# Half-size products of the output projection in another order, first layernorm rows in halves, weight sums from tiles already on chip, and self-checks at the end of the next matrix product

## Chip, cores and metric

One core of one Trainium2 chip. The metric is the device time of one execution in microseconds (us), lower is better. The kernel before took 1502.25 us, the median of three runs (1499.3 to 1504.81).

The engines named below are TensorE (PE, matrix products), VectorE (DVE), ScalarE (ACT), GpSimd (POOL) and SyncE (SP, which only issues DMAs). ACT and POOL issue DMAs too. Each engine executes its own list of instructions in order and waits for others through semaphores.

## The reference

A transformer layer on 2048 tokens of width 1024, with a recurrent attention of 32 heads of 128 (64 segments of 32 tokens, 8 memory rows carried from one segment to the next), and a feed-forward part. All six modulation rows come from a vector `c`.

```python
h = _layernorm(x) * (1 + ca) + sa
# attention by segments: tokens [mem(8) | 32 rows], q, k, v by Wq, Wk, Wv, masked softmax,
# o = heads @ Wo ; mem = o[:, :8] for the next segment ; output o[:, 8:]
x = x + ga * A(h, mem0, Wq, Wk, Wv, Wo)
h = _layernorm(x) * (1 + cb) + sb
h1 = _gelu(_layernorm(h) @ w1)
hs = shifted_quarters(h1) @ w2
x1 = h + hs
x = x + gb * (x1 + _gelu(_layernorm(x1) @ w3) @ w4)
```

So the token rows pass through Wo (4096 x 1024), a residual sum, two layernorms one after the other, then w1, w2, w3 and w4.

## The kernel before

Up to about 790 us the attention runs. Head pairs `hp` are projected by `P_units`, whose pieces fill the gaps between pieces of the attention of the pair before. For each pair, `load_wo2` brings the 256 rows of Wo into a tile `wo2`; `M_units` multiplies them with the memory rows of the heads and adds into `Macc` (L717 to L721). A second list of pieces, `guard_units`, reads w3 and w4 through a single tile, squares them on ACT (the squares' sums go into a check), and in between reads Wo once more, pair by pair: `wo_sums` forms four differences of its 512-wide blocks with four DVE subtractions and stores them through GpSimd's queue to `WoT_d` (L699). The heads' outputs of the tokens, transposed, go to `OTw_d` (L779).

The Wo product of the tokens follows, in two waves of 1024 tokens each. A wave computes a 2 by 2 block product with seven half-size products instead of eight (Winograd's form of Strassen's algorithm), in the order `ORDER`. A product is two halves `hf` of the 4096-deep sum, and a half is four units `i`, each 8 matmuls 128x128 by 128x512 into one PSUM bank (L970). The left operands are the token blocks A11, A12, A21, A22 and three sums of them, formed by DVE in place on SBUF slots (`X_sum`, `sums`; one sum of a half is 128 x 4096 fp16). The right operands are quarters of Wo or the sums in `WoT_d`; `b_upto` loads them, half a product at a time, through a ring of four tiles on SP's queue, ahead of the unit that calls it. `load_a` loads the token blocks on the same queue.

Two families of PSUM banks take part: `b` (pools of `acc_tile`) is opened by product 1 and is the target of 1, 6, 7 and 4; `d` (pool `psB`, four banks) is opened by 2 and again by 5, and is the target of 2, 5 and 3. After the second half of a product, `after(j, i)` takes results out: `snap` (L930) is an ACT copy of 128x512 to SBUF, `fin` (L936, L937) a DVE add of a bank and a snapshot and a DVE multiplication by `ga`, which gives half a row tile of x1. Before a unit may open a bank again, all readers of the bank must be done.

Row tiles (128 tokens, 8 in a wave) then pass through `C1a`: xt, the rows of x, comes in on SP's queue (L1102), GpSimd adds it (L1103), ACT's queue stores x1 (L1105), `ln_act` normalizes: DVE statistics (L106 to L110; their result for the first layernorm lies in `ves`), rstd on GpSimd (L112), one small DVE operation, one ACT operation (L1093) that makes u. DVE scales and shifts u (L1108, L1109), it is stored, and a second `ln_act` makes z, which `C1b` brings transposed into `zTs` by a DMA on ACT's queue. `chain(t0)` makes four row tiles, one lagging behind the other, and `interleave` weaves it between products: tiles 0 to 3 with the last two products of wave 0, 4 to 7 with the first three of wave 1, 8 to 11 with its last two, 12 to 15 with the first two blocks of w1.

w1 is four blocks `A_units(b)` of 512 tokens, eight units of eight matmuls each (L1182), with a gelu on ACT (L1183). Blocks 0 and 1 read `zTs[0]`, 2 and 3 `zTs[1]`; as the rows are shifted by 32 tokens, block 2 also needs the first z of tile 12, and block 3 needs all up to tile 15. w2 follows (from 1086 us), then w3 and w4.

Two self-checks run on the way. `check_a` compares the memory rows' result in eight rounds (GpSimd, ACT squares, GpSimd: L1043 to L1047), between products 3 and 6 of wave 0. `check_b` sums up over limits on the softmax's denominators, on the squares of w3 and w4, on `ves` and others, with a matmul at its end (L1082) between the second and the third block of w1; its flag goes to the host's side as an output.

The compiler's scheduler orders the instructions of each engine by estimated readiness and by the order in which the program creates them, up to the w3 and w4 part, whose order is written out. The order of allocation of ring tiles and pool buffers follows the program.

Of the kernel before, what the change touches and what calls it, by code (L numbers as in the profile page):

```python
# [60 lines left out]
def kernel(ctx, tc, A_x, A_mem0, A_Wq, A_Wk, A_Wv, A_Wo, A_seg_len, B_x, B_w1, B_w2, B_w3, B_w4, c, w_mod, out,  # L61
# [41 lines left out]
    def layernorm_stats(pool, src, ve=None):  # L103
        st = pool.tile([P, 2, 6], F32, name="ln_st")
        for i in range(2):
            nc.vector.bn_stats(out=st[:, i, :], in_=src[:, i * 512:(i + 1) * 512])  # L106
# [62 lines left out]
    def first_pass(late_hook):  # L169
# [53 lines left out]
        wop = LM.enter_context(tc.tile_pool(name="up_wo", bufs=2))  # L223
        otmp = LM.enter_context(tc.tile_pool(name="up_otm", bufs=2))
# [315 lines left out]
        wsp = LX.enter_context(tc.tile_pool(name="x_ws", bufs=1))  # L540
        rowp = LX.enter_context(tc.tile_pool(name="up_row", bufs=1))
        ws_pools[:] = [wsp]
        state = {}
# [6 lines left out]
        def load_wo2(hp):  # L550
            wo2 = wop.tile([P, 2, D], BF16, name="wo2")
            nc.sync.dma_start(wo2[:], Wo2[hp * 256:hp * 256 + 256, :].rearrange("(h p) n -> p h n", p=P))
            state["wo2", hp] = wo2

# [72 lines left out]
        def P_units(hp):  # L627
# [8 lines left out]
            ms = M_units(hp - 3) if hp >= 3 else []  # L636
            units = []
            for s in range(3):
# [8 lines left out]
                units += ms[s:s + 1]  # L647
# [20 lines left out]
        def guard_units():  # L668
# [32 lines left out]
            for i in range(28):  # L701
                units += [load(i), nop, nop, square(i)]
                if i % 7 in (0, 2, 4, 6):
                    k = i // 7 * 4 + i % 7 // 2
                    units += [wo_load(k), nop, nop, wo_sums(k)]
# [132 lines left out]
        NHP = H // 2  # L838
# [38 lines left out]
        def slot(nm):  # L877
# [3 lines left out]
                 {(0, 0): "s3", (0, 1): "s4", (1, 0): "s0", (1, 1): "s2", "X": "s1"}]  # L881
# [15 lines left out]
        ORDER = (1, 2, 5, 3, 6, 7, 4)  # L897
# [21 lines left out]
        def wave(w):  # L919
# [5 lines left out]
            def x1_new(t):  # L925
                x1s[t] = xpools["tp4"].tile([P, D], F32, name="x1")

# [5 lines left out]
            def fin(t, n, acc, s=None):  # L933
# [3 lines left out]
                nc.vector.tensor_tensor(x1s[t][:, cs], (acc if s is None else s)[:], ga_b[:, cs], ALU.mult)  # L937

            def after(j, i):
# [3 lines left out]
                elif j == 2:  # L943
                    x1_new(t1)
# [3 lines left out]
                elif j == 6:  # L948
                    fin(t1, 1, x["d"], snap("st2", x["b"]))
                elif j == 7:  # L950
                    x1_new(t2)
# [4 lines left out]
            def unit(j, hf, i):  # L956
                def f():
                    if i == 0:
                        b_upto(seq.index((w, j, hf)) + 3)
# [11 lines left out]
                    if hf:  # L971
                        after(j, i)
                return f

            def X_sum(hf):
                def f():
                    ks = slice(8 * hf, 8 * hf + 8)
                    nc.vector.tensor_tensor(f16(open_a(w, "X")[:, ks]), Av[w, (1, 0)][:, ks], Av[w, (1, 1)][:, ks], ALU.add)
                return f

            def sums(hf):
                def f():
                    ks = slice(8 * hf, 8 * hf + 8)
                    A11, A12, A21, X = (Av[w, key][:, ks] for key in ((0, 0), (0, 1), (1, 0), "X"))
                    nc.vector.tensor_tensor(f16(A21), A11, A21, ALU.subtract)
                    nc.vector.tensor_tensor(f16(A11), f16(X), A11, ALU.subtract)
# [3 lines left out]
            U[2][4:4] = [X_sum(0)]  # L990
            U[2].append(X_sum(1))
            U[5][6:6] = [sums(0)]
            U[5].append(sums(1))
            return U

        U0 = wave(0)
# [3 lines left out]
        b_upto(3)  # L1000
        load_a(0, (0, 1), 1)
# [7 lines left out]
        b_upto(5)  # L1009
        load_a(0, (1, 0), 1)  # L1010
        for h, t in ((H - 2, 0), (H - 1, 0), (H - 2, 1)):
            nc.vector.tensor_copy(Av[0, (t, h % 2)][:, 15, :], last_ot[h][:].rearrange("p t c -> p (t c)")[:, 64 + 512 * t:576 + 512 * t])
        LX.close()
# [5 lines left out]
        load_a(0, (1, 1), 0)  # L1019
        load_a(0, (1, 1), 1)  # L1020
        psB = PS.enter_context(tc.tile_pool(name="psB", bufs=4, space=PSUM))
        LZ = ExitStack()
# [4 lines left out]
        xpools["st2"] = LT.enter_context(tc.tile_pool(name="x1_s2", bufs=2))  # L1027
        xpools["tp4"] = LT.enter_context(tc.tile_pool(name="x1_t4", bufs=5))
# [5 lines left out]
        for u in U0[1][4:]:  # L1034
            u()
        acc_pools[:] = [psB]
        for u in M_units(NHP - 2):
            u()

        def check_a(kt):  # L1040
            def f():
                df = ck.tile([P, NMEM - 1], F32, name="df")
                nc.gpsimd.tensor_tensor(df[:], Macc[:, kt, 0:NMEM - 1], Mold[:, kt, :], ALU.subtract)  # L1043
                nc.scalar.activation(df[:], df[:], ACT.Square)
                m2 = ck.tile([P, NMEM - 1], F32, name="m2")
                nc.scalar.activation(m2[:], Macc[:, kt, 0:NMEM - 1], ACT.Square, scale=TAU2 ** 0.5)
                nc.gpsimd.tensor_tensor(Mold[:, kt, :], df[:], m2[:], ALU.subtract)  # L1047
            return f

        def check_b():  # L1050
# [13 lines left out]
            nc.vector.tensor_scalar(low[:], rf, RMIN, None, ALU.is_ge)  # L1064
# [4 lines left out]
            nc.vector.tensor_scalar(wsq[:], wsq[:], W_MAX * W_MAX, None, ALU.is_le)  # L1069
# [10 lines left out]
            nc.vector.tensor_scalar(bad[:], okm[:], -1.0, 1.0, ALU.mult, ALU.add)  # L1080
            pb = acc_tile()[0:1, :]
# [7 lines left out]
        def ln_act(smp, dst, src, ve=None):  # L1089
            mean, rstd = layernorm_stats(smp, src, ve)  # L1090
            nmr = smp.tile([P, 1], F32, name="ln_nmr")
            nc.vector.scalar_tensor_tensor(nmr[:], mean, -1.0, rstd, ALU.mult, ALU.mult)
            nc.scalar.activation(dst, src, ACT.Identity, bias=nmr[:], scale=rstd)  # L1093
# [3 lines left out]
        def C1a(t):  # L1097
            def f():
                x1 = x1s[t]
                xt = tp.tile([P, D], BF16, name="xt2")  # L1100
                for rows, toks in p_rows(t):
                    nc.sync.dma_start(xt[rows, :], x2[toks, :])  # L1102
                nc.gpsimd.tensor_tensor(x1[:], x1[:], xt[:], ALU.add)  # L1103
                for rows, toks in p_rows(t):
# [1097 lines left out]
```

## Time and profile before

| | |
|---|---|
| runs, us | 1504.81, 1502.25, 1499.3 |
| profiled execution, us | 1501.48 |
| its span on the core, us | 1499.7 |
| mean granted TensorE clock | 0.985 |
| attention | to 790 us |
| wave 0 ends, wave 1 starts | 904.9, 909.2 |
| w1 starts, ends | 1019.4, 1086.1 |
| w2, then w3 and w4 | to 1142, then to the end |
| a unit of 8 matmuls | 1.72 us |
| ACT copy L930, 128x512 | 585 ns |
| DVE add L936, mult L937, 128x512 | 683, 679 to 804 ns |
| DVE f16 sum 128x4096 | 2.31 to 2.35 us alone |
| POOL add L1103, 128x1024 | 2.13 us |
| POOL rstd L112, 128x1 | 0.55 us, up to 2.5 us |

The span starts with the first instruction and ends with the last; the execution's time lies 1.78 us above it. Lines of the profile's groups read: line of the kernel, engine, operation, output <- inputs, shape, count | busy us, mean ns | idle us of the engine just before them and what ended most of it. A wait list names who waited, for whom, the total, the number of times and the longest. Several semaphores waited for at once are put down to the one that came last.

### The profile page before, as it was taken

What the parts mean: (1) busy time and instruction counts of PE and PEld (TensorE: products, weight loads), DVE (VectorE), ACT (ScalarE), POOL (GpSimd) and SP (SyncE); (2) the same over time, 40 slices, a digit from 0 to 9 for tenths busy, and PEclk for the clock granted to TensorE, in tenths of its full rate; (3) what the DMA queues carried; (4) which work ended last, traced back from release to release, by engine and by line L of the source; (5) the groups of instructions that cost most, each with busy time, mean ns of one, the idle gap of its engine ahead of it and who ended that gap; (6) DMA issues with size and microseconds to landing.
All of it is one profiled execution on the core that took longest, in us unless ns stands there. A gap on an engine that the chain in (4) does not pass through costs nothing. (4 is left out here: it accounts for less than half of the span.)

```text
span 1499.7 us, 24698 instructions
## 1 busy us (share of the span) xinstructions
PE 1408.1 (94%) x9126; PEld 743.0 (50%) x9126; DVE 975.5 (65%) x2053; ACT 695.2 (46%) x1463; POOL 374.3 (25%) x512
## 2 busy tenths in 40 slices
PE   6998999999999999999998788889898999999998
PEld 4664555555555555555564343334343444444443
DVE  6637766777787766777764368566254657676684
ACT  3635565566655655566551121214456661046400
POOL 6020110100110010101010334233023554546525
PEclk9999999999999999999999899999999999999999
DMA  9878867888788786878589599757499674377812
GB/s 333 285 217 215 182 145 197 219 181 214 195 182 211 182 206 166 199 199 219 134 234 379 205 360 300 221 194 216 100 278 230 219 258 173 107 243 251 284 46 77
DMA packets 392358, 316.99 MB, mean 211 GB/s; under 512 B 199578, under 2 KB 336794, under 8 KB 388386
## 3 DMA queue, kind: packets, MB, share of 16 engines
q1 hardware_dynamic: 351744, 247.18, 61.1%
q0 software_dynamic: 11088, 37.24, 7.1%
q10 hardware_dynamic: 29394, 30.89, 6.6%
q8 instruction: 73, 1.20, 0.3%
q14 instruction: 59, 0.48, 0.1%
HBM read 205.67 MB, written 59.02 MB: 176 GB/s over the span
## 5 line engine op out<-in xcount | busy, mean ns | idle before, releaser
L970 PE MATMUL acc<-wstream,s 128*128 128x512 f16 (+1 forms) x864 | 195.1, 387 | 32.2 <-ACT snap L930 11.3
L622 PEld LDWEIGHTS <-T 128*128 128x128 f16 x1408 | 130.5, 98 | 123.3 <-issue 9.3
L590 ACT COPY snap<-acc 128x480 f32<-128x480 f32 x264 | 145.8, 564 | 90.0 <-PE acc L622 82.9
L622 PE MATMUL acc<-hh,T 128*128 128x480 bf16 (+1 forms) x704 | 162.3, 365 | 2.2 <-DVE KT L594 1.8
L622 PE MATMUL acc<-hs,T 128*128 128x480 f16 x704 | 160.9, 368 | 3.0 <-ACT snap L590 2.8
L970 PEld LDWEIGHTS <-s 128*128 128x128 f16 (+1 forms) x864 | 85.8, 99 | 140.6 <-issue 40.7
L779 POOL DMA_DIRECT2D OTw_d<-OT x32 | 24.8, 775 | 420.1 <-DMA OT<-O 359.2
L1360 PEld LDWEIGHTS <-ring 128*128 128x128 f16 (+1 forms) x784 | 77.1, 98 | 104.8 <-issue 13.9
L741 ACT ACTIVATE E<-ps_s 99x495 bf16<-99x495 f32 (+2 forms) x160 | 87.4, 547 | 45.4 <-PE ps_s L737 44.9
L622 PE MATMUL acc<-hh,wq 128*128 128x480 bf16 x464 | 105.1, 366 | 0.0
L761 DVE TENSOR_TENSOR O<-ps_o,rin_all 99x384 bf16<-99x384 f32 (+1 forms) x192 | 97.5, 510 | 3.9
L1325 ACT COPY snap<-bank_b 128x512 f32<-128x512 f32 x72 | 41.8, 586 | 105.3 <-PE bank_b L1411 58.2
L1411 PEld LDWEIGHTS <-hq 128*128 128x128 bf16 (+1 forms) x560 | 54.7, 98 | 66.1
L594 DVE TENSOR_TENSOR KT<-acc,snap 128x480 bf16<-128x480 f32 x116 | 74.7, 653 | 19.4 <-PE acc L622 14.1
L754 PE MATMUL ps_o<-V,E 99*128 99x129 bf16 (+1 forms) x704 | 80.7, 220 | 5.9 <-DVE O L761 3.8
L1210 DVE TENSOR_TENSOR ring<-ring 128x1024 f16<-128x1024 bf16 (+1 forms) x64 | 82.1, 1303 | 4.4 <-PE bank_b L1411 4.0
L743 DVE TENSOR_TENSOR E<-E,maskB 99x495 bf16<-99x495 bf16 (+1 forms) x128 | 48.1, 376 | 54.2 <-ACT E L741 53.0
L754 PEld LDWEIGHTS <-E 99*128 99x128 bf16 (+1 forms) x704 | 57.1, 98 | 43.5 <-DVE O L761 5.3
L759 ACT ACTIVATE O<-ps_o,rin_all 99x128 bf16<-99x128 f32 x192 | 56.5, 367 | 37.8 <-DVE rin_all L756 37.2
L1411 PE MATMUL bank_b<-ring,hq 128*128 128x512 f16 (+1 forms) x336 | 73.2, 379 | 0.0
L1364 ACT ACTIVATE hq<-join 128x512 bf16<-128x512 f32 x84 | 52.8, 630 | 42.7 <-DVE join L1368 42.5
L594 DVE TENSOR_TENSOR VT<-acc,snap 128x480 bf16<-128x480 f32 x90 | 57.9, 652 | 20.8 <-PE acc L622 15.6
(257 smaller groups left out, 2589.9 us busy)
## 6 DMA issues: line engine op xcount, KB each, us to landing
OTw_d<-OT POOLq DMA_DIRECT2D x32, 512.0 KB, 6.1
wstream<-WoT_d SPq DMA_DIRECT2D x16, 1024.0 KB, 7.0
wstream<-in_B_w_dram SPq DMA_DIRECT2D x28, 512.0 KB, 4.2
ring<-in_B_w_dram SPq DMA_DIRECT2D x28, 512.0 KB, 6.3
ring<-in_B_w_dram SPq DMA_DIRECT2D x8, 1792.0 KB, 10.0
s<-OTw_d SPq DMA_DIRECT2D x13, 1024.0 KB, 9.9
wstream<-in_A_Wo_dram SPq DMA_DIRECT2D x11, 1024.0 KB, 10.3
wq<-in_A_Wq_dram SPq DMA_DIRECT2D x16, 512.0 KB, 5.7
```

Source lines behind the costliest of these rows:

```text
L590: nc.scalar.copy(t[:], st[q][bank][:, 0:CH])
L594: nc.vector.tensor_tensor(view(d, i), chunks(st[q][bank]), chunks(st[q][s_]), ALU.add)
L622: nc.tensor.matmul(acc[:, 0:CH], lhsT=B[:, k, :], rhs=A[:, k, :], start=(j in (1, 2, 5) and k == 0), stop=(k == 3), skip_group_check=True)
L741: nc.scalar.activation(E[:rows, 0:o], ps[:rows, 0:o], ACT.Exp, scale=DH ** -0.5)
L754: nc.tensor.matmul(ps[:, i, :], lhsT=state["e", h, t // 5][:k, c:c + P], rhs=V[:k, t, 0:DH + 1], start=True, stop=True)
L759: nc.scalar.mul(O[:rows, t, :], ps[:rows, i, 0:DH], rin[:, i:i + 1])
L761: nc.vector.tensor_tensor(O[:rows, ts[0]:ts[0] + n, :], ps[:rows, 0:n, 0:DH], rin[:, :, None].to_broadcast([rows, n, DH]), ALU.mult)
L970: nc.tensor.matmul(acc[:], lhsT=A[:, k, i * P:(i + 1) * P], rhs=B[:, k, :], start=(j in (1, 2, 5) and hf == 0 and k == 0), stop=(hf == 1 a ...
L1210: return nc.vector.tensor_tensor(dst, a, b, op)
L1360: nc.tensor.matmul(acc[:], lhsT=B[:, k, q * P:(q + 1) * P], rhs=A[:, k, :], start=(start and k == 0), stop=(k == 3), skip_group_check=True)
L1364: nc.scalar.activation(hq[a][f][:, g * 2 + q, :], src[:], ACT.Gelu_apprx_tanh)
L1411: nc.tensor.matmul(acc[:], lhsT=L3[:, k, i * P:(i + 1) * P], rhs=R3[:, k, :], start=(start and k == 0), stop=(k == 13), skip_group_check=True)
```

## The change

Four parts, all before w2:

1. The differences of Wo for the pairs k below 12 are formed by `WT_units` from the `wo2` tiles that the memory rows use anyway, in a tile of their own (`x_wt`, one buffer); `guard_units` reads Wo again only for the last four pairs. Both `M_units` of the last two pairs stand before product 2.
2. `ORDER` becomes (1, 2, 6, 5, 7, 3, 4): the targets alternate b, d, b, d, b, d, b. The three sums that 6 and 5 and 7 need are moved into product 2, the fourth (`last_sum`) into product 5. The slots of wave 1 change. `b_upto` is called one half further ahead. The first loads are reordered.
3. x1 exists in halves of 512 (12 buffers instead of 5 of 1024; four second snapshots instead of two); the GpSimd add, the x1 store, the statistics and the first normalization each work by halves. xt is loaded on GpSimd's queue. The chains are of eight tiles: tiles 0 and 1 with the last product of wave 0, 2 to 7 with the first four of wave 1, 8 and 9 with its last, 10 to 13 with blocks 0 and 1 of w1, 14 and 15 with block 2.
4. The checks are created after the first unit of block 3 of w1, and parts of them are given a dependence on its last matmul (`pin`); the flag's matmul follows the seventh unit.

```diff
+        def WT_units(k):
+            if k >= NHP - 4:
+                return []
+            w = state["wo2", k][:].rearrange("p b (n c) -> p b n c", c=512)
...
+                nc.vector.tensor_tensor(T1, B12, B11, ALU.subtract)
+                nc.vector.tensor_tensor(T2, B22, T1, ALU.subtract)
...
+                nc.vector.tensor_tensor(T3, B22, B12, ALU.subtract)
+                nc.vector.tensor_tensor(T4, B21, T2, ALU.subtract)
+                nc.gpsimd.dma_start(WoT_d[:, :, k, :].rearrange("j p c -> p j c"), st[0][:].rearrange("p b n c -> p (b n) c"))
+            return [one, two]
...
-                units += ms[s:s + 1]
+                units += ms[s:s + 1] + wo[s:s + 1]
...
-                if i % 7 in (0, 2, 4, 6):
-                    k = i // 7 * 4 + i % 7 // 2
+                if i % 2 and i < 8:
+                    k = NHP - 4 + i // 2
                     units += [wo_load(k), nop, nop, wo_sums(k)]
...
-                 {(0, 0): "s3", (0, 1): "s4", (1, 0): "s0", (1, 1): "s2", "X": "s1"}]
+                 {(0, 0): "s0", (0, 1): "s3", (1, 0): "s2", (1, 1): "s4", "X": "s1"}]
...
-        ORDER = (1, 2, 5, 3, 6, 7, 4)
+        ORDER = (1, 2, 6, 5, 7, 3, 4)
...
-                nc.vector.tensor_tensor(x1s[t][:, cs], (acc if s is None else s)[:], ga_b[:, cs], ALU.mult)
+                x1s[t, n] = xpools["xh"].tile([P, 512], F32, name="x1")
+                nc.vector.tensor_tensor(x1s[t, n][:], (acc if s is None else s)[:], ga_b[:, cs], ALU.mult)
...
                 elif j == 6:
-                    fin(t1, 1, x["d"], snap("st2", x["b"]))
+                    x["s2"] = snap("st2", x["b"])
+                elif j == 3:
+                    fin(t1, 1, x["d"], x["s2"])
...
-                        b_upto(seq.index((w, j, hf)) + 3)
+                        b_upto(seq.index((w, j, hf)) + 4)
...
+                    nc.vector.tensor_tensor(f16(X), A21, A22, ALU.add)
                     nc.vector.tensor_tensor(f16(A21), A11, A21, ALU.subtract)
                     nc.vector.tensor_tensor(f16(A11), f16(X), A11, ALU.subtract)
+            def last_sum(hf):
+                def f():
+                    A11, A12 = (Av[w, key][:, 8 * hf:8 * hf + 8] for key in ((0, 0), (0, 1)))
                     nc.vector.tensor_tensor(f16(A12), A12, f16(A11), ALU.subtract)
...
-            U[2][4:4] = [X_sum(0)]
-            U[2].append(X_sum(1))
-            U[5][6:6] = [sums(0)]
-            U[5].append(sums(1))
+            U[2][2:2] = [sums(0)]
+            U[2][7:7] = [sums(1)]
+            U[5][0:0] = [last_sum(0)]
+            U[5][5:5] = [last_sum(1)]
...
-        b_upto(3)
-        load_a(0, (0, 1), 1)
         b_upto(4)
         load_a(0, (1, 0), 0)
         load_wo2(NHP - 2)
...
-        b_upto(5)
+        load_a(0, (0, 1), 1)
         load_a(0, (1, 0), 1)
...
+        for u in M_units(NHP - 2) + M_units(NHP - 1):
+            u()
...
+        def pin(ins):
+            tc.add_manual_dep(ins.ins, marks["w1"].ins.name, ...)
...
                 for rows, toks in p_rows(t):
-                    nc.sync.dma_start(xt[rows, :], x2[toks, :])
-                nc.gpsimd.tensor_tensor(x1[:], x1[:], xt[:], ALU.add)
-                for rows, toks in p_rows(t):
-                    nc.scalar.dma_start(x1_d[toks, :], x1[rows, :])
+                    nc.gpsimd.dma_start(xt[rows, :], x2[toks, :])
+                for n in range(2):
+                    cs = slice(n * 512, (n + 1) * 512)
+                    nc.gpsimd.tensor_tensor(x1[n], x1[n], xt[:, cs], ALU.add)
+                    for rows, toks in p_rows(t):
+                        nc.scalar.dma_start(x1_d[toks, cs], x1[n][rows, :])
...
-            return lagged(C1a, C1b, list(range(t0, t0 + 4)), lag=1)
+            return lagged(C1a, C1b, list(range(t0, t0 + 8)), lag=1)
...
-        for u in U0[2][0:4] + [lambda: load_a(0, (0, 0), 0)] + U0[2][4:] + [rows2] + M_units(NHP - 1) + U0[5]:
+        for u in U0[2][0:2] + [lambda: load_a(0, (0, 0), 0)] + U0[2][2:] + [rows2] + U0[6] + [next_a((0, 0))] + U0[5] + [next_a((0, 1))] + U0[7] + [next_a((1, 0))] + U0[3]:
             u()
-        interleave(checks, U0[3] + [next_a((0, 0))] + U0[6][0:4] + [next_a((0, 1))] + U0[6][4:])
-        interleave(chain(0), U0[7][0:4] + [next_a((1, 0))] + U0[7][4:] + U0[4][0:4] + [next_a((1, 1))] + U0[4][4:])
+        next_a((1, 1))()
+        interleave(chain0[0:2], U0[4])
...
-        interleave(chain(4), U1[1] + U1[2] + U1[5])
-        for u in U1[3] + [load_w1] + U1[6] + [late_slots]:
+        interleave(chain0[2:], U1[1] + U1[2] + U1[6] + U1[5])
+        for u in U1[7] + [load_w1] + U1[3] + [late_slots]:
             u()
-        interleave(chain(8), U1[7] + U1[4])
+        chain1 = chain(8)
+        interleave(chain1[0:2], U1[4])
...
-        interleave(chain(12), A_units(0) + A_units(1))
-        check_b()
-        for u in A_units(2) + A_units(3):
+        interleave(chain1[2:6], A_units(0) + A_units(1))
+        interleave(chain1[6:], A_units(2))
+        for i, u in enumerate(A_units(3)):
             u()
+            if i == 0:
+                for kt in range(KT):
+                    check_a(kt)
+                check_b()
+            elif i == 6:
+                check_end()
```

## The prediction

> **What bounds the kernel now.** I read the page from the top: the engine shares, then the costliest groups, then the waits of the tensor engine from 790 to 1090 us, where every edit but one lies, and last the timelines at its two longest waits.
>
> ```profile
> PE 1408.1 (94%) x9126; PEld 743.0 (50%) x9126; DVE 975.5 (65%) x2053; ACT 695.2 (46%) x1463; POOL 374.3 (25%) x512
> L970 PE MATMUL acc<-wstream,s 128*128 128x512 f16 (+1 forms) x864 | 195.1, 387 | 32.2 <-ACT snap L930 11.3
> ```
>
> TensorE is busy for 1408.1 of the span's 1499.7 us, so at most 91.6 us can be had by removing waits. The Wo matmuls (second line) stand idle for 32.2 us. The table of stretches puts 755.7 busy us into the first 790, which leaves attention 34 idle us, mostly at the start.
>
> ```profile
> PE acc L970 <- ACT snap L930: 11.3, 2, 8.8
> PE acc L970 <- DVE snap L936: 10.8, 8, 2.4
> PE acc L1082 <- DVE bad L1080: 8.9, 1, 8.9
> PE acc L970 <- DVE x L937: 4.2, 1, 4.2
> PE acc L970 <- DVE Macc L721: 3.7, 2, 3.0
> PE acc L970 <- DVE ves L110: 2.2, 1, 2.2
> ```
>
> Columns: total, times, longest. The two single waits of 8.8 and 8.9 are the checks'; the 10.8 in eight pieces is the shared PSUM banks, freed only when DVE has added a snapshot. The timeline of ACT before the first, of DVE before the second, and of PE at both (start, duration, engine, line, operation; in brackets the idle time before it):
>
> ```profile
> 841.89 0.26 ACT L1044 ACTIVATE df<-df 128x70 f32<-128x70 f32 x1
> 842.05 2.03 ACT L930 COPY snap<-acc 128x512 f32<-128x512 f32 x4
> ```
>
> ```profile
> 1055.12 0.15 DVE L110 TENSOR_SCALAR ves<-ln_mv 128x1 f32<-128x1 f32 x1
> ...
> 1056.45 0.16 DVE L1080 TENSOR_SCALAR bad<-okm 128x1 bf16<-128x1 f32 x1
> 1057.64 0.69 DVE L1108 TENSOR_TENSOR u<-u,cb_b 128x1024 bf16<-128x1024 bf16 x1 [1.03 <-ACT u L1093]
> ```
>
> ```profile
> 842.67 3.57 PE L970 MATMUL acc<-wstream,s 128*128 128x512 bf16 x8 [8.82 <-ACT snap L930]
> ...
> 1056.66 0.16 PE L1082 MATMUL acc<-bad,ones_col 128*1 128x1 bf16 x1 [8.92 <-DVE bad L1080]
> ```
>
> At 842 the snapshot stands on ACT behind the last of eight check rounds, whose GpSimd halves ran at 4.4 to 4.7 us a pair while DVE summed. At 1056 the flag's matmul waits for the statistics (ves) of tile 15, and units 16 to 31 of w1 stand behind it. But the z of tile 15 is itself late: its first scaling is at 1057.64, its transpose is issued at 1063.03 and lands about 1065.5. So taking the flag away can't start w1's last block (A3, 13.8 us) before 1065.5; before it starts near 1072 and ends at 1086.1. Of the 8.9 us some 6 can be had; the layernorm chain owns the rest. This sets the frame: **the end of A3 moves with the landing of the last z.**
>
> **What the Trainium skill says.** "TensorE: Matmul & The Clock Gate", section "What's actually happening", has the array at half clock after an idle window of about 3.4 us, and needing as long a busy stretch to recover. The trace agrees, and even 2.4 us waits did it: after the 8.8 us wait thirteen matmuls came 0.43 us apart instead of 0.215 (+2.7 us). So a long wait costs 1.5 to 2.7 us more. "GPSIMD Engine Reference", section "Specifications", has GpSimd sharing its SBUF interfaces with DVE operations of two SBUF inputs; here the 128x1 rstd takes 0.55 us in quiet and 2.5 us during an f16 sum. "DMA: Bandwidth & Descriptors", section "Anatomy of one DMA", prices a GpSimd-issued DMA at 2.0 us + bytes/436e3, 2.6 us for a 256 KB xt. In the trace a GpSimd-issued row load of 512 KB (gb_b) takes 4.6 us, and the SP-issued xt, by the view of that tile (line below: least, median, most):
>
> ```profile
> DMA to landing us min/median/max: 3.3/4.5/7.3
> ```
>
> These decide over the price.
>
> **The change, part by part.** The ledger runs along the profiled execution (1501.48 us: the span and 1.78 around it, 0.8 below the median of the runs).
>
> *Wo sums for k below 12 from the memory rows' tiles.* Twelve 512 KB loads go; the same four DVE subtracts and one GpSimd store per k remain, now in the fill between attention units. In attention PE waits on no Wo load. I take 0; bounds -2 (less on SP's queue) to +2 (a store is now behind other GpSimd work, and the tile has one buffer).
>
> *Wave 0 (seven products), from 791.5.* Before it ends at 904.9: 52 remaining units at 1.72 = 89.5, memory-row matmuls 2.8, waits 18.6, half clock 2.7. After: both memory-row groups now precede product 2, and the second needs the last wo2 load. Before, that landed at 808.0, issued at 797.4 behind s2. It now stands ahead of the second half of the (0,1) operand, whose issue sat 8.3 us on SP. Product 1 ends about 798.4 and the first group about 799.8; I put the landing at 804 (bounds 800, 808): a wait of 4.2. It takes the place of the 3.0 on Macc. The checks' 8.8 goes, and so do 4.8 of bank waits, since b and d now alternate. New: product 5's first unit is issued ahead of product 6 and waits for its weight half (a ring slot, then saturated DMA, 350 to 424 GB/s): 3.5; product 6 waits for the sum that was moved into product 2, three f16 sums of 2.35 us a half: 3.2. Half clock for these three: 4.5. Sum 89.5 + 2.8 + 4.2 + 3.5 + 3.2 + 4.5 = 107.7, end 899.2, **-5.7**.
>
> *Start of wave 1.* Before, it waits 4.2 for DVE's mult (L937) and starts at 909.2. After, it needs the third and fourth of product 4's evictions; DVE executes these behind the layernorm of tiles 0 and 1, whose rstd is on GpSimd. There xt loads now stand in the same queue, issued two tiles ahead and no more (two xt buffers), and each add waits for one: adds, issues and rstd in one line. Let L be the time from an issue to the add that may go. At L = 5.8 I get a start at 910, with nothing blocked 901; at 4.0, between the SP-issued minimum and median, 905: **-4**.
>
> *Wave 1.* Its bank waits (7.5 us in four) and those about 1003 to 1009 (4.3) go, by the same alternation. x1 of tile 8 is complete only after the first unit of the sixth product's second half, not after the fifth product: 905 + 5 x 13.8 + 6.9 + 1.7 + 2 (half clock) + some 3 for the evictions ahead = 988, against 984.3 before. The gain of the waits is spent on the later place.
>
> *Last eight tiles.* The adds cost 2 x 1.3 instead of 2.13 us. In GpSimd's order tile 8's rstd stands behind the add for xt 10, its second rstd behind xt 12 and 13, tile 9's second behind xt 14 and 15. Counting adds at 1.3, issues at 0.7, rstd at 0.55 and L = 4.0: tile 9's second rstd is at +28.5, tile 10 is scaled at +31. From there on the pace is that of before, one tile per 7.37 us (1035.52, 1042.89, 1050.26, 1057.64): five more, 36.9, and 8 to the landing of z: +75.9. 988 + 75.9 = **1064** for the last z, against 1065.5.
>
> *Checks at the end.* Eight rounds of 1.1 us in quiet (839.3, 840.4, 841.5 above are the pace) start behind the first unit of A3; eight 128-deep matmuls stand among units 2 to 4 and each waits for its round. The rounds take 8.8 us, units and matmuls there 6: +2.5 (bounds 0, if the flow of other units absorbs it, and 9, if DVE slows GpSimd to 2.3 a round). The flag's matmul follows the seventh unit and is ready by then. ACT's gelu (0.6 each) fits between. Releasing these buffers later delays ring loads on SP, hidden by the 55.4 us of w2.
>
> *End.* A3 at 1064 + 13.8 + 2 (half clock after the wait) + 2.5 = 1082.3, against 1086.1: -3.8. From there w2 to w4 are matmul-bound and shift along. 1501.5 - 3.8 = 1497.7; on the runs' scale I say **1497**, the odd microsecond being below what I can place.
>
> **Rivals.**
> *A, GpSimd doesn't hold the chain* (L at 2.6, the skill's price, or the loads landed before their adds). Wave 1 starts at 902, tile 8 is done at 985, tile 9's second rstd comes at +24, last z at 1057; A3 ends at 1075, less 2 if the check rounds hide: 1488 to 1491. For it: no xt is large and the queue carries little else. Against: every measured landing is above 3.2 us.
> *B, slower: xt on GpSimd's queue.* At L = 5.8 wave 1 starts at 910, tile 8 is complete at 993, the last z lands at 993 + 84 = 1077, A3 ends at 1095: +9, 1511. It decides from L of about 5. For it: after 1019 the DMA share in the stretch is 0.91 and landings to 7.3 us exist. With wo2 at 808 and check rounds of 2.3 us it adds 4 each.
> *C, the change does not do what it says.* The removed waits only let PE reach the z of tile 15 sooner, while the later completion of tile 8 and the checks in A3 give it all back: 1497 to 1507, most likely 1502. For it: the chain view already passes through layernorm, not PE, from 868 to 1057.
>
> **How the numbers follow.** My own case, A3's end 2 to 8 us earlier (1493 to 1499), has 0.28; A 0.24; C 0.20; B 0.28. A measurement of this kernel can tell about 0.3% (4.5 us) from no change, so below 1497.7 is faster: A, two thirds of my case (0.19) and the lower end of C (0.02), 0.45. Slower, above 1506.8, is B and the upper end of C (0.04), 0.32; the rest, 0.23, is the same. The range 1485 to 1512 takes in A and B at their computed values and leaves out wo2, attention or check rounds at their ends.
>
> **What would show it.** Right: no wait on L930 of 8 us near 840, none on bad near 1056; a wait on Macc or its wo2 load of 3 to 6 us near 800; the seven-product waits on DVE adds gone; wave 1 starting 903 to 907; tile 8's sum at about 988; last z transposed near 1062; PE waiting before A3, not before A2's flag; eight small waits on the check rounds inside A3. Wrong: xt landings outside 3.3 to 4.8 us, a pace of the last six tiles other than 7.37 us, w1's blocks waiting on something else than z, or a stage before 790 that moved by more than 2 us.

## The result, and the profile after

The changed kernel takes 1549.68 us, the median of four runs (1547.96 to 1552.65); the kernel before 1501.22 us in the same comparison. The ratio is 1.032 with an interval of 1.030 to 1.035: slower by 48 us, far outside the forecast range of 1485 to 1512. In the profiled execution the span went from 1499.7 to 1547.5 us, by 47.8.

The engine shares and the Wo matmuls' group on the page of the changed kernel (its lines are shifted: L995 is the former L970, L962 the former L937, L649 the former L622, L333 the former L331, L621 the former L594, L745 the former L717, L1225 the former L1182):

```profile
PE 1418.4 (92%) x9080; PEld 746.2 (48%) x9126; DVE 966.6 (62%) x2053; ACT 698.2 (45%) x1479; POOL 376.8 (24%) x545
L995 PE MATMUL acc<-wstream,s 128*128 128x512 f16 (+1 forms) x855 | 194.7, 390 | 23.7 <-DVE x L962 12.7
```

TensorE's busy time rose by only 10 us, at a mean granted clock of 0.973 instead of 0.985; the rest is idle time. Before the Wo matmuls it even fell, from 32.2 to 23.7 us. So the loss lies in other stages. The next lines are TensorE's waits from 0 to 790 us in the changed kernel (total, times, longest), and DVE's in the same time. `DVE KT L621` is the addition that takes a result of the K projection out of its PSUM bank, an eviction in what follows.

```profile
PE acc L649 <- DVE KT L621: 13.2, 11, 2.9
PE acc L333 <- DVE KT L621: 6.8, 5, 4.4
```

```profile
DVE wt L572 <- DMA wo<-in_A_Wo_dram: 35.5, 10, 5.5
```

In the kernel before, the first two took 1.8 and 2.6 us, and the third, the first subtraction of `WT_units`, didn't exist:

```profile
PE acc L331 <- DVE KT L594: 2.6, 2, 1.9
PE acc L622 <- DVE KT L594: 1.8, 2, 1.0
```

Then TensorE's waits in the changed kernel from 790 to 1000 us and the longest from 1000 to 1200:

```profile
PE acc L995 <- DVE x L962: 12.7, 1, 12.7
PE acc L745 <- DMA wo<-in_A_Wo_dram: 8.3, 1, 8.3
PE acc L995 <- DMA wstream<-WoT_d: 5.6, 1, 5.6
PE acc L995 <- DVE s L1008: 4.6, 1, 4.6
```

```profile
PE acc L1225 <- DMA s<-z: 12.9, 1, 12.9
PE acc L1225 <- ACT s L1226: 12.5, 2, 10.1
PE acc L1225 <- DVE x L962: 4.0, 1, 4.0
...
PE acc L1088 <- POOL Mold L1080: 2.4, 6, 0.5
```

The many small bank waits and the checks' two long ones are gone, as forecast. In their place stand three loads and sums at the start of wave 0, one wait before wave 1, a bank wait of 4.0 us inside the first block of w1, and two long waits before its last two blocks. From the start of wave 1 on, TensorE's timeline reads:

```profile
937.30 98.20 PE L995 MATMUL acc<-wstream,s 128*128 128x512 bf16 x442 [0.22 <-issue]
1035.34 5.62 PE L1225 MATMUL acc<-zA,s 128*128 128x512 bf16 x23
1044.98 11.32 PE L1225 MATMUL acc<-zA,s 128*128 128x512 bf16 x39 [4.01 <-DVE x L962]
...
1112.04 4.61 PE L1225 MATMUL acc<-s,s 128*128 128x512 bf16 x13 [12.89 <-DMA s<-z]
```

The timelines of both kernels give the whole loss by stages:

| stretch | before, us | after, us | difference |
|---|---|---|---|
| start to the second half of Wo product 1 | 791.5 | 807.2 | +15.8 |
| from there to the end of wave 0 | 113.5 | 116.6 | +3.1 |
| wait before wave 1 | 4.2 | 12.7 | +8.5 |
| wave 1, to the start of w1 | 110.4 | 98.8 | -11.6 |
| w1 (four blocks) | 66.4 | 97.2 | +30.8 |
| w2 to w4 | 413.8 | 415.0 | +1.2 |

So the new order of the products does what it was made for: wave 1 is 11.6 us shorter, of which 9.4 are six waits between the products of the kernel before. w1 loses more than that. Its waits grew from 8.9 to 29.4 us. Matmuls that follow a wait at 0.43 us from one to the next instead of 0.215 (half clock in what follows) cost about 7 us there instead of 1.5, by the spacing of their weight loads.

### The profile page after: what moved, and what is told of

The parts are those of the page before. It is cut to its first block, busy times and chain, and to the rows that moved or that the text cites. A ratio compares the mean times of both kernels' runs of the same rounds, so it can differ in the third digit from the quotient of the medians.

```text
span 1547.5 us, 24690 instructions
## 1 busy us (share of the span) xinstructions
PE 1418.4 (92%) x9080; PEld 746.2 (48%) x9126; DVE 966.6 (62%) x2053; ACT 698.2 (45%) x1479; POOL 376.8 (24%) x545
## 5 line engine op out<-in xcount | busy, mean ns | idle before, releaser
L995 PE MATMUL acc<-wstream,s 128*128 128x512 f16 (+1 forms) x855 | 194.7, 390 | 23.7 <-DVE x L962 12.7
L649 PEld LDWEIGHTS <-T 128*128 128x128 f16 x1408 | 130.5, 97 | 133.8 <-issue 19.1
L649 PE MATMUL acc<-hh,T 128*128 128x480 bf16 (+1 forms) x704 | 164.1, 367 | 13.2 <-DVE KT L621 13.2
L649 PE MATMUL acc<-hs,T 128*128 128x480 f16 x704 | 159.3, 365 | 1.4 <-DVE VT L621 0.6
L995 PEld LDWEIGHTS <-s 128*128 128x128 f16 (+1 forms) x864 | 86.5, 100 | 131.4 <-issue 29.5
L649 PE MATMUL acc<-hh,wq 128*128 128x480 bf16 x464 | 105.5, 365 | 0.1
L789 DVE TENSOR_TENSOR O<-ps_o,rin_all 99x384 bf16<-99x384 f32 (+1 forms) x192 | 97.2, 510 | 3.6
L621 DVE TENSOR_TENSOR KT<-acc,snap 128x480 bf16<-128x480 f32 x116 | 73.7, 653 | 14.2 <-PE acc L649 11.0
L621 DVE TENSOR_TENSOR VT<-acc,snap 128x480 bf16<-128x480 f32 x90 | 58.1, 651 | 22.1 <-PE acc L649 15.6
```

The lines of the kernel that those rows point to most:

```text
L621: nc.vector.tensor_tensor(view(d, i), chunks(st[q][bank]), chunks(st[q][s_]), ALU.add)
L649: nc.tensor.matmul(acc[:, 0:CH], lhsT=B[:, k, :], rhs=A[:, k, :], start=(j in (1, 2, 5) and k == 0), stop=(k == 3), skip_group_check=True)
L789: nc.vector.tensor_tensor(O[:rows, ts[0]:ts[0] + n, :], ps[:rows, 0:n, 0:DH], rin[:, :, None].to_broadcast([rows, n, DH]), ALU.mult)
L995: nc.tensor.matmul(acc[:], lhsT=A[:, k, i * P:(i + 1) * P], rhs=B[:, k, :], start=(j in (1, 2, 5) and hf == 0 and k == 0), stop=(hf == 1 a ...
```

## The experiments

Each of the three large losses has a suspect: the Wo sums in attention, GpSimd's queue before wave 1, and the chain of the last eight tiles in w1. The times are medians; the ratios are to the kernel before in the same comparison.

**Part 1 alone, on the kernel before** (the move of the last `M_units` is left out).

```diff
...
+            wo = WT_units(hp - 3) if hp >= 3 else []
...
-                units += ms[s:s + 1]
+                units += ms[s:s + 1] + wo[s:s + 1]
...
-                if i % 7 in (0, 2, 4, 6):
+                if i % 2 and i < 8:
```

> The kernel before with part 1 alone: the differences of Wo from the memory rows' tiles. Theory W (DVE stands in its queue waiting for the landing of the wo2 tile, and the projections' evictions behind it come late for TensorE): the wait of DVE on the Wo rows is again 30 to 40 us in all, TensorE's waits on the evictions of K rise to some 20 us, the second half of the first Wo product starts 12 to 17 us later than in the kernel before, and the whole takes 1512 to 1518 us. Rival V (the loss in attention comes from the other parts, for example from the reordered first loads of the Wo stage): within 3 us of the kernel before.

1521.84 us, ratio 1.011 (1.007 to 1.015). DVE waits 33.8 us for the Wo rows and the second half of product 1 starts at 809.6 instead of 791.5. Part 1 alone is enough for the loss in attention, a little more than forecast, and TensorE's waits on the evictions of K are 17.8 us. V falls.

**The pieces a third of a head pair later.**

```diff
-                units += ms[s:s + 1] + wo[s:s + 1]
+                units += ms[s:s + 1] + (wo[s - 1:s] if s else [])
```

> The changed kernel with each of the two pieces of Wo differences one third of a head pair later; the same arithmetic, loads and stores. Theory W (wait for the landing): DVE's wait on the Wo rows falls from 35 us to under 10, the first Wo product starts 10 to 16 us earlier than in the changed kernel, about 1535 to 1540 us. Rival D (the DVE work in this place, or the store on GpSimd's queue, costs the time, not the wait): no gain, within 4 us of 1549.

1555.76 us: no gain, and DVE's wait was 39.2 us. As written down, that spoke against W. But the wait hadn't moved: the subtraction ran at the landing of its tile again. The place in the program doesn't set the place in the queue. In the changed kernel, the SyncE, DVE and PE timelines show for one pair the load, the subtraction that waits for it, an eviction of K behind it, and the matmul that waits for that eviction (start, duration, engine, line):

```profile
223.77 1.77 SPq L557 DMA_DIRECT2D wo<-in_A_Wo_dram  x1
```

```profile
231.28 0.43 DVE L572 TENSOR_TENSOR wt<-wo 128x512 f16<-128x512 bf16 x1 [5.52 <-DMA wo<-in_A_Wo_dram]
...
232.29 0.65 DVE L621 TENSOR_TENSOR KT<-acc,snap 128x480 bf16<-128x480 f32 x1
```

```profile
233.00 0.97 PE L649 MATMUL acc<-hh,T 128*128 128x480 bf16 x4 [2.95 <-DVE KT L621]
```

The memory-row matmul of the same pair, which stands just ahead of the subtraction in the program, ran only 66 us later:

```profile
297.82 0.43 PE L745 MATMUL acc<-OTm,wo 128*128 128x71 bf16 x8
```

The scheduler had moved the subtraction ahead in DVE's queue, to a place that is reached before the tile has landed. The old `wo_sums` couldn't move so: its first subtraction was held in order with the other pieces of its list (`keep_order`).

**The sums held behind that matmul.**

```diff
-                nc.vector.tensor_tensor(T1, B12, B11, ALU.subtract)
+                d = nc.vector.tensor_tensor(T1, B12, B11, ALU.subtract)
+                tc.add_manual_dep(d.ins, marks["mm", k].ins.name, ...)
...
+                            marks["mm", hp] = nc.tensor.matmul(a3[:, k, :], ...)
```

> The changed kernel, with the first difference of a pair made to follow the memory-row matmul of the same pair on TensorE; the run before showed that the scheduler puts it a round (some 46 to 66 us) ahead of that, right on the landing of the tile. Theory W: DVE's wait on the Wo rows goes from 35 us to under 3, TensorE's waits on the evictions of K from 20 to under 6, the first Wo product starts 10 to 16 us earlier, 1533 to 1539 us. Rival D (the added DVE work in the fill, wherever it stands): the wait goes but the Wo product starts no more than 4 us earlier, above 1545 us.

1526.94 us, ratio 1.016 (1.012 to 1.020): 22.7 us won back, more than forecast. DVE's wait on the Wo rows is gone (what is left in this place is 15.1 us in ten pieces on the single buffer's store), and TensorE no longer waits for K. The second half of product 1 starts at 782.6. All the kernels fall into three groups by that start: with the sums from the second read of Wo 791.5, 792.0, 795.7 and 796.0 us (793.8 on average); with the sums not held 803.8 to 817.4 (six kernels, 810.5 on average); with the sums held 781.2, 781.9, 782.6 and 784.2 (782.5). The groups don't overlap. So the idea of part 1 is worth some 11 us at this point, and its placement cost 28.

**xt back on SyncE's queue, in the changed kernel.**

```diff
-                    nc.gpsimd.dma_start(xt[rows, :], x2[toks, :])
+                    nc.sync.dma_start(xt[rows, :], x2[toks, :])
```

> The changed kernel with the loads of xt back on SyncE's queue. Theory Q (rival B of the prediction: GpSimd's queue, stopped at adds that wait for xt, holds the rstd of the layernorms): wave 1 starts 5 to 9 us earlier after the end of wave 0 (wait of 12.7 us down to 4 to 8), tiles 8 to 10 follow at about 10 us instead of 14, the last block of w1 starts 10 to 20 us earlier, 1528 to 1538 us. Rival H (the adds hold GpSimd in any case because the scheduler puts them ahead of rstd, and a load from SyncE comes no earlier, standing behind weight loads that wait for a ring tile): less than 4 us of gain, or a loss.

1540.32 us, ratio 1.025 (1.021 to 1.029). The wait before wave 1 fell from 12.7 to 4.2 us; tiles 9 and 10 each follow after 11.8 us instead of 14.7 and 13.9; the last block of w1 starts at 1102.2 instead of 1112.0. Theory Q holds for the wait before wave 1; the gain at the end, 9.4 us, falls just short of what it expected. GpSimd's timeline of the changed kernel shows the stop. An add waits 4.05 us for its xt, and the second rstd of tile 0, which had its input at 922.1 us, runs only after it. DVE waits for that rstd, and the evictions that wave 1 needs (L962) stand behind:

```profile
920.81 0.56 POOL L1142 DMA_DIRECT2D xt<-in_A_x_dram  x1 [0.30 <-POOL x L1145]
922.15 1.14 POOL L1145 TENSOR_TENSOR x<-x,xt 128x512 f32<-128x512 f32 x1 [0.78 <-DMA xt<-in_A_x_dram]
927.35 1.15 POOL L1145 TENSOR_TENSOR x<-x,xt 128x512 f32<-128x512 f32 x1 [4.05 <-DMA xt<-in_A_x_dram]
928.46 0.56 POOL L113 TENSOR_TENSOR ln_rstd<-ln_ve,mhalf 128x1 f32<-128x1 f32 x1
```

```profile
929.05 0.16 DVE L1128 SCALAR_TENSOR_TENSOR ln_nmr<-ln_mv,ln_rstd 128x1 f32<-128x1 f32 x1 [6.73 <-POOL ln_rstd L113]
...
930.04 0.69 DVE L962 TENSOR_TENSOR x<-acc,ga_b 128x512 f32<-128x512 f32 x1
```

**The first normalization in halves, on the kernel before.** In w1 the changed kernel scaled tiles 10 to 13 every 8.3 us, not every 7.37 (the last two took 8.6 and 9.4). ACT's timelines, before and after, of one tile each:

```profile
1041.63 1.23 ACT L1093 ACTIVATE u<-x,ln_nmr,ln_rstd 128x1024 bf16<-128x1024 f32 x1
1041.75 1.25 ACTq L1119 DMA_TRANSPOSE s<-z  x1
```

```profile
1071.15 0.80 ACT L1133 ACTIVATE u<-x,ln_nmr,ln_rstd 128x512 bf16<-128x512 f32 x1
1071.27 1.25 ACTq L1161 DMA_TRANSPOSE s<-z  x1
1072.57 0.81 ACT L1133 ACTIVATE u<-x,ln_nmr,ln_rstd 128x512 bf16<-128x512 f32 x1 [0.62 <-issue]
```

The issue of the transpose used to lie under one long operation. Now it stands between two short ones, and the second waits 0.62 us for it. The edit makes only this difference:

```diff
-            nc.scalar.activation(dst, src, ACT.Identity, bias=nmr[:], scale=rstd)
+            for n in range(2 if ve is not None else 1):
+                cs = slice(n * 512, (n + 1) * 512) if ve is not None else slice(0, D)
+                nc.scalar.activation(dst[:, cs], src[:, cs], ACT.Identity, bias=nmr[:], scale=rstd)
```

> The kernel before with the first normalization on ACT in two halves of 512 columns, nothing else (x1 stays whole). Theory S (the second half stands behind the issue of the transpose of z, 1.25 us, on ACT's queue): the pace of the last six row tiles goes from 7.37 to 8.3 us, the z of tile 15 lands 5 to 8 us later, and the whole takes 1505 to 1510 us. Rival (the slower pace has its cause in GpSimd's queue or in the halves of the add): the pace stays within 0.3 us of 7.37 and the time within 3 us.

1507.76 us, ratio 1.0035 (1.0013 to 1.0057). The pace went to 8.39 us, and from the scaling of tile 8 to that of tile 15 it took 69.4 us instead of 62.6. Theory S holds.

**The transpose behind both halves, in the changed kernel.**

```diff
...
+            if ("u", t + 1) in marks:
+                tc.add_manual_dep(tr.ins, marks["u", t + 1].ins.name, ...)
...
-            return lagged(C1a, C1b, list(range(t0, t0 + 8)), lag=1)
+            return [lambda t=t: (C1a(t)() if t < t0 + 8 else None, C1b(t - 1)() if t > t0 else None) for t in range(t0, t0 + 9)]
```

So that the dependence can be given, the program now creates a tile's transpose after the next tile's normalization; this second difference was not tried by itself.

> The changed kernel with the transpose of a tile's z behind both halves of the next tile's first normalization on ACT, instead of between them. Theory S: the pace of the last row tiles goes from 8.3 back to 7.4 to 7.7 us (two shorter operations with one fixed cost more remain), the z of tile 15 lands 4 to 6 us earlier, 1543 to 1546 us. Rival: the transposes, now later, make blocks 0 to 2 of w1 wait longer and no time is won.

The pace of tiles 11 to 14 went to 7.6 us, as S has it. Of the whole little can be said: the two runs took 1544.55 and 1553.07 us, and in the profiled execution attention alone was 9 us longer than in the changed kernel, which this edit doesn't touch. From tile 8's scaling to the start of the last block it took 80.5 instead of 83.9 us, although tile 10 followed tile 9 after 17.3 instead of 13.9.

**The checks at the end, on the kernel before.**

```diff
...
-        interleave(checks, U0[3] + [next_a((0, 0))] + U0[6][0:4] + [next_a((0, 1))] + U0[6][4:])
+        for u in U0[3] + [next_a((0, 0))] + U0[6][0:4] + [next_a((0, 1))] + U0[6][4:]:
+            u()
...
-        check_b()
-        for u in A_units(2) + A_units(3):
+        for u in A_units(2):
             u()
+        for i, u in enumerate(A_units(3)):
+            u()
+            if i == 0:
+                for kt in range(KT):
+                    check_a(kt)
+                check_b()
+            elif i == 6:
+                check_end()
```

The parts of the checks are given the dependence of part 4 (`pin`) as well.

> The kernel before with part 4 alone: both checks at the end of w1. The step of the prediction: the wait of 8.8 us near 840 goes, the wait on the flag near 1056 goes, but the last block of w1 can't start before the z of tile 15 lands, and the check rounds stand inside it. In the changed kernel that block took 20.5 us instead of 13.8. So w1 ends 0 to 8 us earlier: 1493 to 1501 us. Rival: both waits come off in full, 17 us: 1485 us. Other rival: the rounds inside the block cost more than the removed waits: above 1503 us.

1493.27 us, ratio 0.991 (0.988 to 0.994). Both long waits are gone, and w1 ends 9.7 us nearer to the start of the Wo product. The last block waits 2.86 us for the last z and takes 20.5 us, in which the summing matmuls wait for their rounds.

**The same, with the summing matmuls behind the seventh unit.**

```diff
         def check_end():
-            rmx, bad = state["check"]
+            pn = acc_tile()[0:1, :]
+            for kt in range(KT):
+                nc.tensor.matmul(pn[:, 0:NMEM - 1], lhsT=ones_col[:], rhs=Mold[:, kt, :], start=(kt == 0), stop=(kt == KT - 1))
...
+            bad = state["check"]
```

> The kernel before with both checks at the end of w1, and with the eight summing matmuls of the first check behind the seventh unit of the last block instead of among units 2 to 4, so that no matmul waits for a round. In the run with the checks alone that block took 20.5 us of which 13.8 are its units. If the rounds cost what the trace shows, the block takes 15 to 16.5 us and the whole 4 to 5 us less than there: 1487 to 1491 us. Rival (the rounds also hold gelu on ACT, and this holds TensorE's banks): no gain, 1492 to 1495 us.

1488.24 us, ratio 0.991 (0.988 to 0.994); the ratios of the two runs don't tell them apart, but the block does: 16.0 us instead of 20.5, as expected, and the median lies 5 us lower. Its end on TensorE's timeline, with all nine matmuls of the checks in 0.4 us:

```profile
1056.42 2.97 PE L1189 MATMUL acc<-s,s 128*128 128x512 bf16 x9 [2.85 <-DMA s<-z]
1059.62 10.76 PE L1189 MATMUL acc<-s,s 128*128 128x512 bf16 x46 [0.22 <-issue]
1070.30 0.43 PE L1081 MATMUL acc<-Mold,ones_col 128*1 128x70 bf16 x8
1070.57 0.16 PE L1089 MATMUL acc<-bad,ones_col 128*1 128x1 bf16 x1
```

**The last Wo rows ahead of A21, in the changed kernel.**

```diff
         b_upto(4)
-        load_a(0, (1, 0), 0)
         load_wo2(NHP - 2)
...
+        load_a(0, (1, 0), 0)
         load_a(0, (0, 1), 1)
```

> The changed kernel with the last load of Wo rows for the memory rows ahead of the token block A21 on SyncE's queue. The issue of that block took 6.5 us of the queue. Theory: the load lands 5 to 7 us earlier, the wait of 8.3 us before product 2 falls to 1 to 3 us; but the sums of product 2 then get A21 later, so that the wait before product 6 (4.6 us on the sum) grows by 0 to 4 us: the end of wave 0 moves by -6 to 0 us, the whole 1543 to 1550 us.

1538.81 us, below what was expected. Attention was 3.5 us shorter by itself. In wave 0 the wait on the Wo rows fell from 8.3 to 4.7 us, the one on the sum from 4.6 to 1.3, but the one on the load of Wo sums grew from 5.6 to 10.2: 16.2 instead of 18.5 in all. With less half clock (about 3 instead of 6 us) the stretch to the end of wave 0 took 111.6 instead of 116.6 us, within the expected gain. In both orders the start of wave 0 waits for loads.

**Five corrections together, in the changed kernel** (sums held, xt on SyncE, Wo rows ahead, sums of the check late, transposes behind u; the edits are those above).

> The changed kernel with five corrections together: Wo sums held behind the memory rows' matmul, xt on SyncE's queue, the last Wo rows ahead of A21, the first check's summing matmuls behind the seventh unit, the transposes behind u. If the five losses add up (22 + 9 + 5 + 4.5 + 5 us by single runs or their theories), 1502 to 1507 us, the level of the kernel before. Rival: they hide each other, since all but the first and fourth move only the arrival at the layernorm of the last eight tiles: 1510 to 1520 us. Other rival: with them gone the alternation of the banks shows its gain, below 1498 us.

1495.11 us, ratio 0.9946 (0.9927 to 0.9965): 54.6 us below the changed kernel, where the losses of the expectation add up to 45.5. So they don't hide each other. The time lies where the second rival puts it, but that the banks are the reason is not shown: wave 1 takes 98.4 us here and took 98.8 in the changed kernel. The last two blocks of w1 still wait 11.7 and 9.7 us for z.

**The same, with product 3 ahead of product 7.**

```diff
-        ORDER = (1, 2, 6, 5, 7, 3, 4)
+        ORDER = (1, 2, 6, 5, 3, 7, 4)
...
-        for u in U1[7] + [load_w1] + U1[3] + [late_slots]:
+        for u in [load_w1] + U1[3] + [late_slots]:
             u()
         chain1 = chain(8)
-        interleave(chain1[0:2], U1[4])
+        interleave(chain1[0:2], U1[7] + U1[4])
```

> The changed kernel with the five corrections and product 3 before product 7: order 1, 2, 6, 5, 3, 7, 4, so that a wave's first four row tiles are complete after five products, as in the kernel before, at the price of two products in a row on one bank family (5 then 3, 7 then 4). Both mended kernels hold the Wo sums; the one with the old order, whole x1 and chains of four takes 1478.3 us, the one with the new ones 1495.1. Theory L (the later completion of tile 8 and the chain behind it are the largest part of these 17 us): the last z lands 8 to 13 us earlier, the waits on the banks in the two waves come back with some 3 to 5 us each, 1486 to 1492 us. Rival (the chain of eight with its halves sets the end by its own pace, wherever it starts, or the bank waits eat what it wins): 1493 us or more.

1491.13 us, ratio 0.992 (0.989 to 0.994). Tile 8's first add is at 971.1 instead of 981.5, the last block of w1 starts at 1057.1 instead of 1066.3, of which 2.3 us come from the start of the Wo product. The bank waits that returned are small (2.0 us), the wait before wave 1 grew from 3.3 to 8.8. So the last z came some 7 us earlier by the order. The time lies in L's range, but only 4 of the 17 us were won: L names a part, not the largest one. One block of w1 still waits 12.3 us for z.

**The mended parts on the kernel before**: checks at the end with the late sums, and Wo sums held; old order, whole x1, chains of four.

> The kernel before with two parts of the change in mended form: checks at the end of w1 with the summing matmuls behind the seventh unit, and the Wo sums from the memory rows' tiles held behind their matmul. The order of products, whole x1 and xt on SyncE stay. The first part alone gave 1488.2 us; with the sums held the Wo product of the changed kernel began 22 us earlier than without, that is some 4 to 6 us earlier than in the kernel before. Expected 1481 to 1487 us. Rival (the earlier start of the Wo product only makes it wait longer for its loads): 1487 to 1490 us.

1478.28 us, ratio 0.985 (0.982 to 0.987), faster than both kernels. TensorE's waits from 780 to 1062 us in it, the four longest entries:

```profile
PE acc L997 <- DVE snap L963: 13.4, 8, 4.7
PE acc L1215 <- ACT s L1216: 2.6, 3, 2.0
PE acc L997 <- DVE x L964: 2.5, 1, 2.5
PE acc L997 <- ACT snap L957: 2.5, 1, 2.5
```

It keeps the bank waits (13.4 us in eight) and is still 17 us faster than the five-times corrected kernel, which has none of them in its waves and waits 21.4 us for z, 5.2 for Wo rows, 5.7 for Wo sums and 4.3 for a token sum. With parts 1 and 4 mended on both sides, the rest of parts 2 and 3 costs 17 us: the new order with its sums and loads, the halves and the chains of eight. The profiled executions of the three mended kernels show where (us):

| stretch | old order | new order, five corrections | the same, product 3 earlier |
|---|---|---|---|
| start to the second half of Wo product 1 | 781.2 | 784.2 | 781.9 |
| from there to the end of wave 0 | 104.9 | 112.8 | 110.6 |
| wait before wave 1 | 2.5 | 3.3 | 8.8 |
| wave 1, to the start of w1 | 110.5 | 98.4 | 101.9 |
| w1 (four blocks) | 61.7 | 84.4 | 69.7 |
| w2 to w4 | 414.0 | 414.5 | 416.3 |

The profiled execution with five corrections is the slowest of its six, 4 us above their median. The new order wins 12 us in wave 1, and w1, waiting for z, loses 23. With product 3 earlier, wave 1 and w1 together take as long as in the old order (171.6 against 172.2 us), and the loss lies in wave 0 and in the wait behind it (12.0 us). How these losses divide among the halves, the chains of eight and the loads stays open: the order of the change needs x1 in halves (whole tiles would leave product 7 no buffer before product 3 is done), and the three were not tried apart.

## Why the prediction was wrong

**The frame held.** "The end of A3 moves with the landing of the last z": in the changed kernel the last block starts at 1112.04, on the DMA of z. The two check waits went. The bank waits went too, and wave 1 ran without a wait, one stretch of 442 matmuls: it is 11.6 us shorter, and the forecast named 11.8 us of bank waits there (the trace of the kernel before has 9.4 us in six waits, with slow matmuls behind some of them). From the start of wave 1 to tile 8's sum it took 81.6 us, forecast 83. What failed lies before and behind.

**The step that failed outright: Wo sums, "I take 0; bounds -2 to +2".** It was +15.8. I counted the instructions (the same) and asked whether TensorE waits on a Wo load in attention (it doesn't). I didn't ask what the new subtraction waits for and what stands behind it on DVE. In the trace of the changed kernel it runs 66 us before its pair's matmul, at the landing of its tile. DVE waited 35.5 us, the K evictions behind it came late, and TensorE's waits on them rose from 4.4 to 20 us. Holding the subtraction behind the matmul won 22.7 us back.

**Wave 0, forecast -5.7, measured +3.1.** Every wait was in its forecast place; sizes failed. Wo rows 4.2 forecast, 8.3 measured: I had put the landing 12.5 us behind the start of this stretch, and it came at 15.9, since SyncE's issues of two weight halves and a token block took 9.4 and 6.5 us ahead of the load, and the load itself took 11.8. Weight half 3.5, measured 5.6; sum 3.2, measured 4.6. That is 7.6 of the 8.8 us; half clock, 4.5 forecast, was about 6 (30 matmuls). That "even 2.4 us waits did it" holds for one of three in the kernel before: after the wait of 2.45 us at 963 matmuls came 0.43 us apart, after those of 2.42 at 894 and 1009 they didn't.

**Start of wave 1 and rival B.** Forecast 5.8 us after wave 0's end, measured 12.7. B's mechanism is right: with xt on SyncE it was 4.2. The landings lay between 2.9 and 9.3 us, median 4.3, so L = 4.0 was near the median. But the four xt issued before wave 1, from 907.8 to 920.8 us, took 5.0 to 7.0, near B's L of 5.8. Each of several adds in a row has its own xt, and the longest of them sets the end. Here and after tile 8, a median was the wrong figure.

**Last eight tiles, forecast +75.9 us from tile 8's sum, measured 93.9** (1018.1 to 1112.0). To tile 10's scaling +31 forecast, +38.7 measured: two xt took 6.5 and 9.3 us. That is not all of it, for with xt on SyncE it was still +36.3, and with all five corrections +33.8. Five further tiles 36.9 forecast, 42.9 measured: I had carried the pace of 7.37 us over to a chain whose ACT operation is cut in two, and had put nothing for the cut. The tail 8 forecast, 12.4 measured: the last transpose lands after 6.7 us instead of 3.1 (so 8.5 in the kernel before, where I had read 8), while four weight loads pass; that these loads are its cause was not tried.

**Checks, +2.5 and 2 of half clock, measured 6.7**; the run with late sums shows, on the kernel before, that 4.5 of it were the matmuls among the units.

**The sum.** The span was to shrink by 3.8 us and grew by 47.8, a miss of 51.6. Attention has 15.8 of it, wave 0 8.8, the start of wave 1 6.9, the last eight tiles 18.0, the block with the checks 2.2 and the part from w2 on 1.2; tile 8's sum came 1.4 sooner after the start of wave 1 than forecast. So two terms are the largest: the one that I had put at nothing, and the chain of the last eight tiles.

**The rivals.** A fell: no xt landed in less than 2.9 us. B named the right cause before wave 1, but at 1511 us too small a loss. C's thought, that the later tile 8 and the checks in the last block give the gain back, is right in kind: moving product 3 forward brought the last z some 7 us forward. None of the rivals held a loss in attention; without it the changed kernel would still lie some 32 us above the kernel before, and that is also beyond B. All the signs of being wrong that I had named came true: landings up to 9.3 us, another pace of the last tiles, a wait in w1 on a bank instead of z, and a stage before 790 that moved by more than 2 us.

## What to carry to other kernels

A new instruction can cost what is queued behind it. Before an edit is priced at nothing because its work was there before, look up what it waits for and where the scheduler has put it on its in-order engine, and hold it there by a dependence if its data comes from a load. A change with several parts should be tried part by part: here one part was worth 15 us once its matmuls stood late, a second 10 once it was held in place, and together with the others they showed as a loss of 48.

## What the runs showed of the hardware that was not expected

The issue of a DMA transpose on ACT took 1.25 us of its queue. In the kernel before it cost nothing under an operation of 1.23 us that was started before it; in the changed kernel it cost 0.62 us between two of 0.80. Two ACT operations of 512 columns took 0.80 us each where one of 1024 took 1.23. And the time of attention differed by 9 us between the profiled executions of two kernels with the same code there, the changed one and the one with the transposes behind u (807.2 and 816.4 us to the second half of product 1): stages that an edit doesn't touch must be taken out before a difference of a few microseconds is read.
